# The last spectral block's sums on the PSUM banks of the side that was idle

## The chip, the core and the metric

The kernel runs on one core of one Trainium2 chip. The metric is the device time of one execution in microseconds (us); the time of a kernel is the median of several executions. Everything is float32, and large products are made as three products of a rounded part and a remainder ("hi" and "lo"), which the code calls `products` or writes out as `(hi, a), (hi, a's lo), (lo, a)`.

## What is computed

The input x has 2048 rows of 512 numbers. Two mixers read it and a gate blends them:

```python
g = sigmoid((x * gate_w).sum(-1, keepdims=True))
a = softmax(q @ k.T * scale) @ v, over 32 heads of 16, then @ wo     # A: attention
b = real(DFT_seq(DFT_hidden(x)))                                       # B: spectral
  = dft_seq_re @ (x @ dft_hid_re.T) - dft_seq_im @ (x @ dft_hid_im.T)
out = g * a + (1 - g) * b
```

## The kernel before, in words

The program has a front and a loop. The **front** projects x to queries, keys and values, makes the two spectral operands x @ dft_hid, and then multiplies them by the sequence matrices, one block of 128 output rows after the other. Beside this work it scans scores: for the softmax it needs the row maxima of q @ k.T, and the function `beside()`, called after every step of the front, puts a scan between the products at a chosen pace. The **loop** then runs over 16 pairs of heads with 32 steps each: scores, exp, and the product with the values.

The order of instructions on each engine is the order in which the code is written (nothing reorders it); waits are put in by the tile layer, which knows which tile lies where. TensorE (PE) is one stream in order: what waits there holds everything behind it. A step of the front is one pair of matmuls, one on rows 0 to 63 of the array and one on rows 64 to 127 (`halves_of`, L203), which run together and write to two PSUM banks.

PSUM has 8 banks, and in the front they are split so. Four of them on the right (numbers 4 to 7) hold scans. Once the front has reached its folded scans these are four tiles d0, d1, k0, k1 of one bank each. A folded scan (`scan_folded`, L172) writes one bank per half; of its two scores blocks ScalarE (ACT) copies one with Relu to SBUF (`fold`, L176) and VectorE (DVE) later reads the other with it and takes the maximum (L178). The bank is free for a new scan when ACT or DVE has read it.

The other four (numbers 0 to 3) hold the sums of the blocks, as two **sides** of two banks: side 0 and side 1. The function `xy()` gives each new block the other side: `turns[0] += 1; side = turns[0] % 2`. While block n accumulates on one side, block n-1 on the other is read out by ACT: `tx` (L767, one bank) and `ty` (the other bank), each multiplied by 1 - g. The read of `ty` is put 5 steps later for most blocks (L316); for the last block but one of the spectral part it stands straight behind `tx` (L769). From 12 to 44 steps after the end of a block the idle side serves as a third place for scans (`spare`, `bed`); after the last block but one it does not.

At the last spectral block the pool of the sides (`pxy`) is closed and the loop's pool (`psf`) takes the same four banks. The loop's pool has two tiles of two banks, `wide(0)` and `wide(1)`:

```python
if n == len(coef) - NU:
    sides.close()
    psf.append(ctx.enter_context(tc.tile_pool(name="psf", bufs=1, space=PSUM, ...)))
if u == 0:
    pss[t] = xy(n == len(coef) - NU)      # joined: wide(side)
```

A pool lays its tiles in PSUM in the order in which their tags are first asked for. The last block is side 0 by the count of turns (the code asserts it), so it asks for `wide(0)` first and gets banks 0 and 1. In the front the first call of `xy()` gives side 1, so in `pxy` side 1 lies on banks 0 and 1 and side 0 on banks 2 and 3. The last block but one is on side 1. In the last block the loop's first steps are already interleaved (`go_ahead`, at steps 30, 31, 37 and 44 of the 48): a memset of the sum bank, two scores blocks for exp and one scan; those that need two banks take `wide(1)`, banks 2 and 3.

Of the kernel before, what the change touches and what calls it, by code (L numbers as in the profile page):

```python
# [53 lines left out]
SCANS_IN = 0  # L54
# [12 lines left out]
def build(tc, xT, wqkv, wo, wrT, wiT, cr, ci, ct, gate, out):  # L67
    nc = tc.nc
    with ExitStack() as ctx:
# [199 lines left out]
        with ExitStack() as pf:  # L269
# [9 lines left out]
            def side_bank(side, j, name):  # L279
                return pxy.tile([P, 512], F32, tag=f"side{side}{j}", name=name)  # L280
# [126 lines left out]
            sides, banks = ExitStack(), ExitStack()  # L407
            pxy = sides.enter_context(tc.tile_pool(name="pxy", bufs=1, space=PSUM, reuse_waits="tile"))
            pss1.append(banks.enter_context(tc.tile_pool(name="pss1", bufs=2, space=PSUM, side="right")))

            def begin_folds():

                banks.close()
                psk.append(ctx.enter_context(tc.tile_pool(name="psk", bufs=1, space=PSUM, side="right", reuse_waits="tile")))
                beds.extend((bed, fp))
                scan_at(BESIDE)
# [941 lines left out]
```

## Time and profile before

| | us |
|---|---|
| median of 3 runs (lowest, highest) | 1718.13 (1718.02, 1718.69) |
| profiled execution, its own time | 1716.91 |
| its span, first to last instruction | 1715.1 |
| PE busy | 1701.1 |
| ACT busy | 1493.0 |
| DVE busy | 1186.8 |
| mean granted PE clock | 0.998 |

The front takes the first 665 us of the span, the loop the rest. In the rows of the profile a line is engine, line of the code, operation, written tile <- read tiles; bracketed at the end stand the engine's idle time before it and what ended it. Matmuls overlap, so the durations of PE rows (0.40 us for a single one) are longer than the distance between starts, and the distance is what counts. PEld is the load of the stationary operand of a matmul. PEclk is the clock granted to PE as a share of full speed.

### The profile page before, as it was taken

Reading aid. Unit: us, or ns where it says so; the run is one execution under the profiler, and the core shown is the slowest. Engines: PE = TensorE matmul, PEld = TensorE weight load, DVE = VectorE, ACT = ScalarE, POOL = GpSimd, SP = SyncE. Lnnn points to the kernel's source line nnn. Section 1 sums busy time; section 2 is a strip of 40 time slices with the busy share of each in tenths; the row PEclk is TensorE's granted clock in tenths of the full one; section 3 lists DMA queues with packets and bytes.
Section 4 is the critical chain, followed back from the end, with each engine's and each line's share of the span. In section 5 each row is a group of like instructions: output and inputs, shape, how many; then the busy total and the mean of one; then the engine's idle time right before and its main releaser. Section 6 shows DMA issues by size and latency. Waiting matters only on the chain.

```text
span 1715.1 us, 36307 instructions
## 1 busy us (share of the span) xinstructions
PE 1701.1 (99%) x13560; PEld 1030.1 (60%) x13560; DVE 1186.8 (69%) x2179; ACT 1493.0 (87%) x2472; POOL 765.0 (45%) x909
## 2 busy tenths in 40 slices
PE   9999999999999999999999999999999999999998
PEld 6988888988888795433333333333345555555554
DVE  5898888889899996666666666666642455654343
ACT  6447889888888887999999999999998888888876
POOL 3672435755555762433535455353422333334222
PEclk9999999999999999999999999999999999999999
DMA  7783457533337664256444445343436465575733
GB/s 255 243 289 76 149 161 216 161 112 107 104 110 204 175 134 95 83 131 153 136 112 113 121 114 135 99 124 85 93 76 145 131 149 148 140 172 157 192 93 127
DMA packets 148962, 240.96 MB, mean 140 GB/s; under 512 B 50049, under 2 KB 60785, under 8 KB 142193
## 3 DMA queue, kind: packets, MB, share of 16 engines
q1 hardware_dynamic: 133520, 217.27, 46.5%
q0 software_dynamic: 14688, 20.33, 5.0%
q8 instruction: 106, 1.74, 0.5%
q10 hardware_dynamic: 576, 1.05, 0.2%
q14 instruction: 72, 0.58, 0.1%
HBM read 158.34 MB, written 81.01 MB: 140 GB/s over the span
## 4 chain that ended last, share of the span: by engine, by line
PE 98%; ACT 0%; DMA 0%; DVE 0%; issue 0%; SPq 0%; DVEq 0%; ACTq 0%
PE pvb L804 29%; PE xy L203 26%; PE s L228 19%; PE s L172 9%; PE s L203 9%; PE s L153 5%; DMA raws<-wqkv 0%; PE s L593 0%; DVE y L919 0%; ACT fold L176 0%; DVE fold L178 0%; SPq L563 0%; SPq L562 0%; ACT ty L316 0%; PE s L1306 0%
## 5 line engine op out<-in xcount | busy, mean ns | idle before, releaser
L252 ACT ACTIVATE eb<-s 128x1024 f32<-128x1024 f32 x512 | 581.1, 1135 | 59.6 <-PE s L228 59.5
L260 ACT ACTIVATE e<-s 128x512 f32<-128x512 f32 x1022 | 610.6, 711 | 0.0
L155 DVE TENSOR_REDUCE mx<-s 128x2 f32<-128x1024 f32 x380 | 460.9, 1224 | 196.8 <-PE s L153 196.5
L804 PE MATMUL pvb<-eb,va 128*17 128x512 f32 x2052 | 514.4, 597 | 0.0
L804 PE MATMUL pvb<-e,va 128*17 128x512 f32 x2044 | 513.5, 597 | 0.0
L178 DVE CUSTOM_DVE_ANT_0 fold<-s,fold 128x512 f32<-128x512 f32 x644 | 433.2, 690 | 59.9 <-PE s L172 34.0
L176 ACT ACTIVATE fold<-s 128x512 f32<-128x512 f32 x644 | 377.8, 603 | 83.9 <-PE s L172 64.0
L228 PEld LDWEIGHTS s<-qs,ks 50*128 50x128 f32 x2048 | 214.6, 184 | 361.7 <-ACT eb L252 269.4
L228 PE MATMUL s<-qs,ks 50*128 50x512 f32 x2048 | 424.0, 435 | 0.0
L203 PE MATMUL xy<-b,c 64*128 64x512 f32 x2448 | 393.5, 394 | 2.0 <-ACT ty L769 1.7
L172 PE MATMUL s<-ks,qs 48*128 48x512 f32 x1288 | 315.2, 403 | 1.3 <-DVE mx L178 0.9
L203 PEld LDWEIGHTS xy<-b,c 64*128 64x128 f32 x2448 | 289.1, 187 | 29.2 <-POOL c L402 2.1
L172 PEld LDWEIGHTS s<-ks,qs 48*128 48x128 f32 x1288 | 171.6, 185 | 35.8 <-DVE mx L178 9.6
L804 PEld LDWEIGHTS pvb<-eb,va 128*17 128x17 f32 x2052 | 69.8, 96 | 188.8 <-issue 179.5
L153 PE MATMUL s<-ks,qs 48*128 48x512 f32 x760 | 156.0, 394 | 0.0
L203 PE MATMUL s<-b,b 64*128 64x512 f32 x1050 | 136.6, 391 | 0.0
L823 POOL DMA_DIRECT2D r_d<-lc x31 | 18.0, 580 | 264.6 <-DVE lc L822 216.9
L203 PE MATMUL xy<-w,b 64*128 64x512 f32 x768 | 115.0, 392 | 0.0
L816 POOL DMA_DIRECT2D lc<-ob x124 | 63.1, 515 | 115.9 <-DVE ob L813 110.6
L203 PEld LDWEIGHTS s<-b,b 64*128 64x128 f32 x1050 | 100.2, 185 | 23.6 <-issue 1.0
L403 POOL TENSOR_TENSOR c<-craw,c 128x512 fp32r<-128x512 f32 x84 | 110.2, 1312 | 6.7
L825 POOL DMA_DIRECT2D rb<-r_d x124 | 60.6, 496 | 102.0 <-DMA r_d<-lc 96.2
(149 smaller groups left out, 1563.1 us busy)
## 6 DMA issues: line engine op xcount, KB each, us to landing
qs<-q_d SPq DMA_DIRECT2D x68, 256.0 KB
craw<-cr SPq DMA_DIRECT2D x60, 256.0 KB
craw<-ct SPq DMA_DIRECT2D x48, 256.0 KB
ks<-k_d SPq DMA_DIRECT2D x46, 256.0 KB
kept_None<-sum SPq DMA_DIRECT2D x40, 256.0 KB
craw<-kept_None SPq DMA_DIRECT2D x40, 256.0 KB
qs<-q_d SPq DMA_DIRECT2D x68, 128.0 KB
craw<-ci SPq DMA_DIRECT2D x32, 256.0 KB
```

The costliest lines, as they stand in the source:

```text
L153: nc.tensor.matmul(ps[:, j, :], qs[b:b + 48, qb * P:(qb + 1) * P], ks[b:b + 48, c * 512:(c + 1) * 512], start=True, stop=True)
L155: nc.vector.tensor_reduce(mx[p][:, :, qb, c], ps, axis=AX.X, op=ALU.max)
L172: nc.tensor.matmul(ps, qs[b:b + 48, qb * P:(qb + 1) * P], ks[b:b + 48, c * 512:(c + 1) * 512], start=True, stop=True)
L176: nc.scalar.activation(fold[j], ps, AF.Relu)
L178: nc.vector.tensor_tensor_reduce(out=fold[j], in0=ps, in1=fold[j], scale=1.0, scalar=-3.0e38, op0=ALU.add, op1=ALU.max, accum_out=mx[p][:, ...
L203: nc.tensor.matmul(ps[j], lhs[r], rhs[r], start=first, stop=last)
L228: nc.tensor.matmul(pss[j], ks[b:b + 50, kb * P:(kb + 1) * P], qs[b:b + 50, q0:q0 + 512], start=True, stop=True)
L252: nc.scalar.activation(e, ps, AF.Exp, scale=SCALE)
L260: nc.scalar.activation(e[j], pss[j], AF.Exp, scale=SCALE)
L403: sub(lo, raw, hi.bitcast(F32))
L804: nc.tensor.matmul(pvb[r:r + VC, :], va[:, kb, 2 * p + j, :], es[c][j], start=kb == 0, stop=kb == NB - 1, tile_position=(0, r))
L816: nc.gpsimd.dma_start(lc[32 * n:32 * n + 32, :], ob[r + DH:r + VC, :].rearrange("p (s e) -> p s e", e=16))
```

## The change

Two lines are added where the front's pools are opened. They ask once for the two tiles of side 0 (SCANS_IN is 0), under a name that nothing writes or reads:

```diff
             pxy = sides.enter_context(tc.tile_pool(name="pxy", bufs=1, space=PSUM, reuse_waits="tile"))
             pss1.append(banks.enter_context(tc.tile_pool(name="pss1", bufs=2, space=PSUM, side="right")))
+            for j in range(2):
+                side_bank(SCANS_IN, j, "laid")
 
             def begin_folds():
```

with

```python
def side_bank(side, j, name):
    return pxy.tile([P, 512], F32, tag=f"side{side}{j}", name=name)
```

With that side 0 lies on banks 0 and 1 for the whole front and side 1 on banks 2 and 3. No instruction is added, removed or moved on any engine. Where the last block begins, the tile that its sums take over is no longer the one of the block just ended (side 1) but that of the block before it (side 0). All lines behind the two new ones have a number higher by two.

This is PE's stream before where the last block begins. `s` is a scan's bank, `xy` a block's sums, `b` a spectral operand, `c` a coefficient block; `Activation`, `DVE` and `Pool` are the semaphores of ACT, DVE and POOL. The second row is the last product of the block before, the third is the first of the last block.

```order
L172 MATMUL s<-ks,qs 128x512 [waits Activation_49]
L203 MATMUL xy<-b_9769,c 128x512 x2
L203 MATMUL xy<-b_9127,c 128x512 [waits Activation_49,Pool_49]
L203 MATMUL xy<-b_9127,c 128x512
L203 MATMUL xy<-b_9128,c 128x512 x2
L172 MATMUL s<-ks,qs 128x512
L172 MATMUL s<-ks,qs 128x512 [waits DVE_49]
L203 MATMUL xy<-b_9127,c 128x512 [waits Pool_49]
L203 MATMUL xy<-b_9127,c 128x512
L203 MATMUL xy<-b_9168,c 128x512 x2
L172 MATMUL s<-ks,qs 128x512 [waits DVE_49]
L172 MATMUL s<-ks,qs 128x512
```

The same place with the change:

```order
L172 MATMUL s<-ks,qs 128x512 [waits Activation_49]
L203 MATMUL xy<-b_9771,c 128x512 x2
L203 MATMUL xy<-b_9129,c 128x512 [waits Pool_49]
L203 MATMUL xy<-b_9129,c 128x512
L203 MATMUL xy<-b_9130,c 128x512 x2
L172 MATMUL s<-ks,qs 128x512 [waits Activation_49]
L172 MATMUL s<-ks,qs 128x512 [waits DVE_49]
L203 MATMUL xy<-b_9129,c 128x512 [waits Pool_49]
L203 MATMUL xy<-b_9129,c 128x512
L203 MATMUL xy<-b_9170,c 128x512 x2
L172 MATMUL s<-ks,qs 128x512 [waits DVE_49]
L172 MATMUL s<-ks,qs 128x512 [waits Activation_49]
```

The wait of the last block's first matmul for ACT (it was for `ty`, L769) is gone. The scan in the sixth row and the one in the last row now wait for ACT in their own name: for the copy that last read the scan's bank, which in the program before is older than `ty` and so was covered by the wait for it. These three rows of PE are all that differs in the program; on the other engines every row and every wait is the same.

## The prediction

> **What bounds the kernel now.** I read the page first: the busy times and the chain that ended last.
>
> ```profile
> PE 1701.1 (99%) x13560; PEld 1030.1 (60%) x13560; DVE 1186.8 (69%) x2179; ACT 1493.0 (87%) x2472; POOL 765.0 (45%) x909
> PE 98%; ACT 0%; DMA 0%; DVE 0%; issue 0%; SPq 0%; DVEq 0%; ACTq 0%
> ```
>
> PE carries the end: the chain runs through it for 98% of the span, and of 1715.1 us it idles 14. A change that removes one wait can pay only where PE itself waited. So the view of PE's waits was next (engine, line, what it waited for: us in total, times, longest).
>
> ```profile
> PE xy L203 <- ACT ty L769: 1.7, 1, 1.7
> PE s L172 <- DVE mx L178: 0.9, 3, 0.5
> ```
>
> The first row is the wait that the change takes out: it occurs once, and it is the longest single wait that PE has for another engine. Next I looked at its surroundings in stretches. The columns are the stretch, its length, then each engine's busy us with its instructions, PE's granted clock, the DMA share and GB/s.
>
> ```profile
> 636.00:646.20 10.20, 10.20 (x91) 8.40 (x88) 9.45 (x29) 8.33 (x14) 5.27 (x6) 1.00 0.77 109
> 646.20:648.20 2.00, 0.35 (x4) 0.00 (x0) 0.96 (x4) 1.81 (x4) 1.48 (x2) 1.00 0.35 69
> 648.20:649.40 1.20, 1.12 (x9) 1.09 (x11) 0.00 (x0) 0.14 (x1) 1.20 (x2) 0.92 1.00 355
> 649.40:652.40 3.00, 3.00 (x17) 2.82 (x15) 1.88 (x5) 1.65 (x3) 1.73 (x2) 0.50 0.31 120
> 652.40:656.00 3.60, 3.60 (x32) 3.04 (x28) 2.98 (x10) 2.40 (x4) 0.00 (x0) 0.97 0.11 39
> 656.00:664.00 8.00, 8.00 (x69) 7.56 (x71) 3.02 (x6) 2.70 (x5) 0.00 (x0) 1.00 0.01 2
> ```
>
> The reader is to see the clock, third column from the right. It is full before the stall and through it, and about 1 us after PE starts again it falls to 0.50 for some 3 us. So the stall has a second price: matmuls that run at half speed after it. PE's own rows show both.
>
> ```profile
> 645.22 0.40 PE L172 MATMUL s<-ks,qs 48*128 48x512 f32 x2
> ...
> 645.92 0.41 PE L172 MATMUL s<-ks,qs 48*128 48x512 f32 x2
> 646.16 0.40 PE L203 MATMUL xy<-b,c 64*128 64x512 f32 x2
> 648.28 0.74 PE L203 MATMUL xy<-b,c 64*128 64x512 f32 x4 [1.73 <-ACT ty L769]
> 648.82 0.44 PE L172 MATMUL s<-ks,qs 48*128 48x512 f32 x2
> ...
> 649.79 0.70 PE L172 MATMUL s<-ks,qs 48*128 48x512 f32 x2
> ...
> 651.07 0.70 PE L172 MATMUL s<-ks,qs 48*128 48x512 f32 x2
> ...
> 652.35 0.56 PE L172 MATMUL s<-ks,qs 48*128 48x512 f32 x2
> ...
> 653.17 0.43 PE L172 MATMUL s<-ks,qs 48*128 48x512 f32 x2
> ...
> 655.50 0.93 PE L172 MATMUL s<-ks,qs 48*128 48x512 f32 x3
> 655.94 1.21 PE L203 MATMUL xy<-b,c 64*128 64x512 f32 x7
> ```
>
> From 645.22 to 645.92 PE does three pairs (one of a scan, two of the block): 0.70 us, so 0.235 us a pair. The scans of the last block should follow each other at that 0.705; after the stall their distances are 0.97, 1.28, 1.28 and 0.82.
>
> **The change, part by part.** The two new calls issue nothing, so they cost nothing, on any queue; the only tiles whose place differs are the blocks' sums and the scans lent to their sides, and they change places with each other. What remains is one wait of PE.
>
> *Taken away, the stall.* The pair at 646.16 would be followed at 646.40 by the next; it came at 648.28. That is 1.88 us. It need not wait for anything else there: side 0 had no scan in the last 4 steps of the block before, and the coefficient it reads was prepared three units earlier.
>
> *Taken away, the slow clock.* Against 0.705 the four distances hold 0.27 + 0.58 + 0.58 + 0.12 = 1.53 us.
>
> [...]
>
> *Added, waits of the scans.* The stall also let ACT and DVE catch up; without it they become the limit for a while. ACT's rows, at an earlier end of a block and at this one:
>
> ```profile
> 632.14 0.71 ACT L316 ACTIVATE ty<-xy,gm 128x512 f32<-128x512 f32 x1
> 632.71 3.21 ACT L176 ACTIVATE fold<-s 128x512 f32<-128x512 f32 x5
> ...
> 642.84 4.14 ACT L176 ACTIVATE fold<-s 128x512 f32<-128x512 f32 x6 [0.31 <-PE s L172]
> 646.88 0.68 ACT L767 ACTIVATE tx<-xy,gm 128x512 f32<-128x512 f32 x1
> 647.45 0.69 ACT L769 ACTIVATE ty<-xy,gm 128x512 f32<-128x512 f32 x1
> 649.26 0.60 ACT L176 ACTIVATE fold<-s 128x512 f32<-128x512 f32 x1 [1.12 <-PE s L172]
> ```
>
> `tx` starts at 646.88 behind a fold, so it stays there, and so does `ty` at 647.45. Without the stall the first scan of the last block runs at 646.40 + 2 x 0.235 = 646.87, the second at 647.57; the ACT copies that they newly wait for are the last two of the six that begin at 642.84 and end at 646.98, so these two waits cost nothing. The third scan, due at 648.28, reuses the first one's banks: its fold follows `ty` after 0.57 (as 632.14 to 632.71), at 648.02, and ends 0.60 later at 648.62. ACT to PE takes 0.14 (`ty` ends at 648.14, PE starts at 648.28), so this scan starts at 648.76, 0.48 late. From there DVE is the chain:
>
> ```profile
> 630.92 0.69 DVE L178 CUSTOM_DVE_ANT_0 fold<-s,fold 128x512 f32<-128x512 f32 x1
> ...
> 634.06 0.69 DVE L178 CUSTOM_DVE_ANT_0 fold<-s,fold 128x512 f32<-128x512 f32 x1
> ...
> 646.46 0.69 DVE L178 CUSTOM_DVE_ANT_0 fold<-s,fold 128x512 f32<-128x512 f32 x1
> ...
> 649.41 0.69 DVE L178 CUSTOM_DVE_ANT_0 fold<-s,fold 128x512 f32<-128x512 f32 x1 [2.25 <-PE s L172]
> ...
> 653.01 0.69 DVE L178 CUSTOM_DVE_ANT_0 fold<-s,fold 128x512 f32<-128x512 f32 x1 [0.40 <-PE s L172]
> ...
> 655.18 0.69 DVE L178 CUSTOM_DVE_ANT_0 fold<-s,fold 128x512 f32<-128x512 f32 x1
> 655.93 0.18 PEld L172 LDWEIGHTS s<-ks,qs 48*128 48x128 f32 x1 [0.40 <-DVE mx L178]
> ```
>
> When it is fed without gaps DVE takes three of these in 2.17 us (653.01 to 655.18), 0.72 each. DVE is idle from the fold at 646.46 to the one at 649.41, the last block's first. The last scan of the front, at 655.93, waits for the block's seventh, the one at 655.18. Without the stall the second fold decides: it needs ACT's copy that ends at 648.62, so it starts at 648.66 (the first has run before, from 647.3 on). Five more distances of 0.72 bring the seventh to 652.26; it lasts 0.69, and with 0.15 to PE the last scan starts at 653.1. With no wait of PE at all it would start after 17 pairs of the block and 8 of scans: 646.40 + 25 x 0.235 = 652.28. So the new waits hold 0.8 us, spread over 6 us in pieces of at most 0.5.
>
> *The sum.* 655.93 - 653.1 = **2.8 us** earlier; by terms, 1.88 (stall) + 1.53 (clock) + 0.2 (what the old wait at 655.93 held) - 0.8 (new waits). The bounds: 655.93 - 652.28 = 3.65 if ACT and DVE are never late; and 2.5 if DVE goes at the slower pace that it had behind the end of the block before, four distances in 3.14 us (630.92 to 634.06), 0.785 each, which puts the seventh fold 0.33 later. I take 2.8, since its durations are those of the same place.
>
> *What carries it to the end.* From 655.94 on PE runs 8.00 of 8.00 us, so the block's end moves by the same amount. The loop then:
>
> ```profile
> 659.96 1.03 ACT L252 ACTIVATE eb<-s 128x1024 f32<-128x1024 f32 x1 [3.35 <-PE s L228]
> ...
> 663.90 1.02 ACT L252 ACTIVATE eb<-s 128x1024 f32<-128x1024 f32 x1 [1.94 <-PE s L228]
> ...
> 666.26 1.02 ACT L252 ACTIVATE eb<-s 128x1024 f32<-128x1024 f32 x1 [0.35 <-PE s L228]
> ...
> 700.00:800.00 100.00, 100.00 (x742) 38.15 (x740) 67.57 (x63) 100.00 (x160) 45.59 (x61) 1.00 0.49 129
> ```
>
> ACT enters it waiting for PE three times, and is busy without a gap later (100.00 of 100 us), so its stream of exps starts earlier by what PE is earlier. The first two banks of the loop now lie where `ty` was read; that read ends at 648.14, and PE needs them at about 656.5. Nothing gives the 2.8 us back.
>
> The profiled execution took 1716.91 us and its span 1715.1; it would take 1714.1. The median of the runs lies 1.22 above it, and the same difference from 1718.13 gives **1715.3 us**. A measurement of this kernel tells about 0.2%, 3.4 us, from no change, so this forecast counts as no change by a little.
>
> **The rivals.**
>
> *More: the drop of the clock is larger in the timed runs.* The profiled execution is 1.22 us faster than their median. If that is a longer drop behind the same stall, the change removes it too: 2.8 + 1.2 = 4.0, 1714.1 us. For it: nothing else in the program waits by chance at a cost of this size. Against it: a profiled execution can differ in other ways.
>
> *Less: in the timed runs the clock does not drop.* Then PE goes at 0.235 from 648.28 and DVE decides before as well: from its first fold at 649.41 six distances of 0.72 lead to the seventh at 653.73, and 0.69 + 0.15 later, at 654.57, the last scan starts. The gain is 654.57 - 653.1 = 1.5: 1716.6 us. [...]
>
> *Slower: the loop's first scores wait for their rows.* The first exp's scores now start near 656.5, and they need rows whose loads were issued by the queue up to 646. If those landed late, PE would wait there; it is a loss over 0.2% if they land later than 659.3 + 3.4 = 662.7.
>
> ```profile
> 654.00:656.00 2.00, 2.00 (x20) 1.59 (x16) 1.81 (x6) 1.41 (x3) 0.00 (x0) 1.00 0.01 4
> ```
>
> The DMA share is 0.01 by 654, so they have long landed. A chance of 0.03.
>
> *Nothing: the span does not follow PE's start,* or the removed wait was not the one that held PE: 1718.1 us.
>
> **How the numbers follow.** The forecast (2.5 to 3.65 us less) 0.55; larger drop 0.22; no drop 0.15; slower 0.03; nothing 0.05. Over 0.2% faster are the larger drop and the upper tail of the forecast (0.10): 0.32. Slower 0.04 with 0.01 for what I don't see. The rest, 0.64, is within. The range goes from the larger drop with 0.2 of spread, 1713.9, to the case without a drop with 0.3, 1716.9; outside lie slower, nothing, and a part of the larger drop, some 0.15 together.
>
> **What would show it.** In the new profile the wait of PE for `ty` is gone from PE's waits; PEclk is 1.00 in every stretch from 636 to 664; the third scan of the last block waits about 0.5 us for ACT's fold and the last one for DVE; the first exp starts at about 657.2 instead of 659.96, and the span is about 1712.3. I am wrong if PE stalls again within the block for more than 1 us, if the clock drops all the same, or if the exp stream starts earlier and the span doesn't follow.

## The result, and the profile after

The changed kernel takes 1714.35 us (median of 22 executions, 1713.49 to 1715.53) and the kernel before 1717.01 us (22 executions beside them, 1715.36 to 1718.69). The ratio is 0.9986 with a 95% interval of 0.998 to 0.9992: a gain of 2.7 us, which is clear of the scatter and below 0.2%. Forecast were 1715.3 us and a gain of 2.8; the 1715.3 were counted from 1718.13, the median of three, and the same gain counted from 1717.01 is 1714.2. The profiled execution's span is 1712.4 us; 1712.3 was forecast.

PE's waits after, all that the view lists:

```profile
PE s L580 <- POOL ident masks.py:199: 1.4, 1, 1.4
PE s L172 <- DVE mx L178: 0.9, 3, 0.4
PE s L1308 <- DVE rb L1305: 0.9, 1, 0.9
PE s L172 <- ACT fold L176: 0.6, 2, 0.4
PE xy L203 <- ACT c L371: 0.3, 1, 0.3
PE xy L203 <- DVE b L372: 0.2, 1, 0.2
```

The wait for `ty` is gone, and a scan that waits for ACT's fold has come. The same stretches as before the change (stretch, length, busy us of each engine with its instructions, PEclk, DMA share, GB/s):

```profile
646.20:648.20 2.00, 2.00 (x20) 1.59 (x16) 1.73 (x6) 1.86 (x5) 1.41 (x2) 1.00 0.05 6
648.20:649.40 1.20, 0.95 (x10) 0.49 (x6) 0.68 (x2) 1.10 (x4) 1.20 (x2) 1.00 0.57 171
649.40:652.40 3.00, 3.00 (x29) 2.52 (x27) 2.93 (x11) 2.57 (x5) 1.86 (x2) 1.00 0.52 194
```

PE is busy through the place of the stall and the clock is full in all of it: where the kernel before did 17 matmuls in 3.00 us, 29 are done. PE, DVE and ACT in order of time:

```profile
646.22 0.87 PE L203 MATMUL xy<-b,c 64*128 64x512 f32 x6
646.92 0.40 PE L172 MATMUL s<-ks,qs 48*128 48x512 f32 x2
...
647.62 0.41 PE L172 MATMUL s<-ks,qs 48*128 48x512 f32 x2
...
648.74 0.50 PE L172 MATMUL s<-ks,qs 48*128 48x512 f32 x2 [0.25 <-ACT fold L176]
...
653.01 3.69 PE L203 MATMUL xy<-b,c 64*128 64x512 f32 x28
656.32 0.61 PE L228 MATMUL s<-qs,ks 50*128 50x512 f32 x2
```

```profile
648.72 0.69 DVE L178 CUSTOM_DVE_ANT_0 fold<-s,fold 128x512 f32<-128x512 f32 x1 [0.52 <-ACT fold L176]
...
652.25 0.69 DVE L178 CUSTOM_DVE_ANT_0 fold<-s,fold 128x512 f32<-128x512 f32 x1
```

```profile
657.03 1.03 ACT L252 ACTIVATE eb<-s 128x1024 f32<-128x1024 f32 x1 [3.35 <-PE s L228]
...
660.96 1.02 ACT L252 ACTIVATE eb<-s 128x1024 f32<-128x1024 f32 x1 [1.93 <-PE s L228]
...
663.31 1.02 ACT L252 ACTIVATE eb<-s 128x1024 f32<-128x1024 f32 x1 [0.35 <-PE s L228]
```

The third scan starts at 648.74, DVE's second fold at 648.72 and its seventh at 652.25, the front's last scan goes with the row at 653.01, and the first exp starts at 657.03 instead of 659.96. The three waits of ACT at the loop's entry are those of before (3.35, 1.93, 0.35), only 2.9 us earlier.

One measure serves for all that follows, since the front of an execution can end up to 0.9 us later than in another: the time from the last pair of the block before to the first scores of the loop. It is 659.29 - 646.16 = 13.13 us before and 656.32 - 646.22 = 10.10 us after.

### The profile page after: what moved, and what is told of

Read it like the earlier page. It is cut to its first block, busy times and chain, and to the rows that moved or that the text cites. A ratio compares the mean times of both kernels' runs of the same rounds, so it can differ in the third digit from the quotient of the medians.

```text
span 1712.4 us, 36306 instructions
## 1 busy us (share of the span) xinstructions
PE 1701.0 (99%) x13560; PEld 1022.5 (60%) x13560; DVE 1188.9 (69%) x2179; ACT 1492.3 (87%) x2472; POOL 765.4 (45%) x909
## 4 chain that ended last, share of the span: by engine, by line
PE 97%; DMA 1%; DVE 0%; issue 0%; ACT 0%; SPq 0%; DVEq 0%; ACTq 0%
PE pvb L806 29%; PE xy L203 26%; PE s L228 19%; PE s L172 9%; PE s L203 8%; PE s L153 5%; DMA q_d<-eh 0%; DMA raws<-wqkv 0%; DMA raws<-xT 0%; PE s L595 0%; DVE y L921 0%; DVE fold L178 0%; ACT fold L176 0%; SPq L565 0%; SPq L564 0%
## 5 line engine op out<-in xcount | busy, mean ns | idle before, releaser
L203 PEld LDWEIGHTS xy<-b,c 64*128 64x128 f32 x2448 | 284.0, 187 | 30.5 <-issue 1.0
```

What stands on the lines that cost most here:

```text
L203: nc.tensor.matmul(ps[j], lhs[r], rhs[r], start=first, stop=last)
```

## The experiments

My theory: what counts is which block's banks the last block takes over, and the stall that this causes is paid twice, as idle time and as a slower clock. The rivals: the new place of the sides pays by itself; the clock falls for another reason; what is left of waits is PE's own pace.

### Which part of the new placement counts

The loop's two tiles can be laid in the other order, with the change (e1) and without it (e2):

```diff
     psf.append(ctx.enter_context(tc.tile_pool(name="psf", ...)))
+    wide(1 - SCANS_IN, "laid")
```

> The changed kernel, with the loop's two tiles laid in the other order too, so that the last block's sums again lie on the banks of the block just ended (now banks 2 and 3). My theory (what counts is which block's banks the last block takes over): PE waits 1.7 us for ty again, the clock falls to 0.50 behind it for about 3 us, the first exp starts at about 660.0 us of the span, the span is about 1715.1 and the time that of the kernel before, ratio 1.000. Rival (where the sides lie in the front pays in itself): the time of the changed kernel, ratio 0.9985.

> The kernel before, with only the loop's two tiles laid in the other order: the front's sides stay where they were, the last block takes banks 2 and 3, those of side 0. My theory: the same as the changed kernel, no wait for ty, PEclk 1.00 all through, first exp at about 657.0, span 1712.4, ratio 0.9985. Rival (the front's placement pays): the kernel before, span 1715.1, ratio 1.000.

e1 took 1716.96 us (ratio to the kernel before 0.9999, 0.999 to 1.0008), e2 1714.82 us (0.999, 0.9981 to 0.9998). So the front's placement pays nothing by itself that these intervals show, and the loop's order alone does what the change does. e2's measure is 657.02 - 646.91 = 10.11 us, as after; its span is 1713.0 us where 1712.4 was expected, and its front ended 0.7 us later than the changed kernel's (646.91 against 646.22). e1 has the wait back:

```profile
PE xy L203 <- ACT ty L772: 1.7, 1, 1.7
```

but not all of the expectation came true. Its clock:

```profile
646.20:648.20 2.00, 0.52 (x6) 0.09 (x2) 1.12 (x4) 1.85 (x4) 1.30 (x2) 1.00 0.05 6
648.20:649.40 1.20, 0.96 (x8) 0.96 (x10) 0.00 (x0) 0.10 (x1) 1.20 (x2) 1.00 0.54 117
649.40:652.40 3.00, 3.00 (x29) 2.78 (x27) 2.72 (x8) 2.55 (x5) 1.83 (x2) 1.00 0.62 216
```

The same stall of 1.7 us, and in this execution the clock did not fall; by their mean clock 5 of e1's 11 executions lost it. Its measure is 657.87 - 646.31 = 11.56 us. Against 13.13 in the kernel before, 1.57 us are the price of the fall when it happens; against 10.11, 1.45 us are the price of the stall without it. Whether the clock falls differs from one execution to the next.

### How often the clock falls, and what decides it

Each execution has its mean granted clock. At the span's end PE idles and the clock falls in every trace, 1.9 to 5.3 us before the last instruction, so an undisturbed execution shows 0.999 (at the far end of that range 0.998), and one fall of 3.4 us more makes 0.998 or 0.997 of it. The rounding makes single cases uncertain, but few: of the 77 executions of the changed kernel, e2, e4, e5 and e8, none of which has the stall of 1.7 us, one shows 0.998. Of the 80 executions of the kernel before that ran beside the experiments, 44 show 0.998 or 0.997, with a median of 1717.7 us, and 36 show 0.999, with a median of 1716.3 us. They ran on two chips: 33 of 65 on one, and 11 of 15 on the one that e7 below ran on. Of the 33 of the changed kernel (22, and 11 as e9 below) none is below 0.999.

The first try to measure the clock's part by itself put seven extra pairs of matmuls ahead of the last block, to keep PE busy while it would wait:

```diff
     psf.append(ctx.enter_context(tc.tile_pool(name="psf", ...)))
+    busy = wide(1 - SCANS_IN, "busy")
+    for _ in range(7):
+        halves_of((busy[:, 0, :], busy[:, 1, :]), hi[:, 0, :], ah[0], True, True)
```

> The kernel before with seven extra pairs of matmuls ahead of the last block (7 x 0.235 = 1.65 us, on the loop's other tile, read by nobody), so that PE is busy while it would wait for ty. It measures the clock's part by itself. My theory (the idling makes the clock fall): PE waits only about 0.2 us for ty, PEclk stays 1.00, the last block starts at 648.3 as before, the front's last scan at about 654.6 instead of 655.9, first exp at about 658.6, span about 1713.7, so 1.4 us of the 2.8 come without any change of banks, ratio 0.9992. Rival (the clock falls there for another reason, or its fall costs nothing): PEclk 0.50 again, last scan at 655.9, span 1715.1, ratio 1.000.

It missed by its own construction: the extra tile was asked for first, so it, and not the block, got the banks of the block just ended, and the extra pairs waited for `ty`.

```profile
PE busy L203 <- ACT ty L772: 1.7, 1, 1.7
649.40:652.40 3.00, 3.00 (x17) 2.90 (x16) 0.28 (x1) 0.48 (x1) 1.60 (x2) 0.50 0.50 188
```

1717.52 us (1.0003, 0.9994 to 1.0012): the stall stayed and work was added. It shows again that the first tile asked for takes the stall. It does not part the clock from the stall: the clock fell as in the kernel before, in 5 of 11 executions by the mean. Put right, with the block's tile laid first:

```diff
     psf.append(ctx.enter_context(tc.tile_pool(name="psf", ...)))
+    wide(SCANS_IN, "laid")
+    busy = wide(1 - SCANS_IN, "busy")
+    for _ in range(7):
+        halves_of((busy[:, 0, :], busy[:, 1, :]), hi[:, 0, :], ah[0], True, True)
```

> The filler of e3 put right: the tile of the last block is laid first, so the seven extra pairs write banks 2 and 3, which are idle, and wait for nothing. The block still waits for ty, but PE is busy for 1.65 us of that time. My theory (idling makes the clock fall in a part of the executions, here never): every execution has a mean clock of 0.999, none of 0.998; their times lie where the undisturbed half of the kernel before lies, median about 1715.8; 11.5 us from the last pair of the block before to the first scores of the loop, like e1, whose clock did not fall. Rival (the clock falls there by chance of another kind): about half of the executions at 0.998 and above 1716.8.

1715.57 us (0.9991, 0.9982 to 1.0): 1.3 us below the median of the kernel before beside it (1716.83), with more work and the same late start of the block; the interval reaches 1.0. One execution took 4081.99 us, for a cause that the record does not show; without it the median is 1715.51. PE's rows in the filled stall, then the stretch behind it and the stretch at the span's end (columns as in the other stretches):

```profile
647.03 0.40 PE L203 MATMUL xy<-b,c 64*128 64x512 f32 x2
647.27 1.77 PE L203 MATMUL busy<-b,c 64*128 64x512 f32 x14
649.07 0.74 PE L203 MATMUL xy<-b,c 64*128 64x512 f32 x4
...
658.55 0.58 PE L228 MATMUL s<-qs,ks 50*128 50x512 f32 x2
649.40:652.40 3.00, 3.00 (x28) 2.42 (x25) 2.12 (x7) 1.95 (x4) 2.66 (x3) 1.00 0.00 0
1708.99:1714.25 5.26, 0.00 (x0) 0.00 (x0) 0.14 (x1) 0.00 (x0) 0.01 (x1) 0.50 0.67 250
```

The measure is 11.52 us, as in e1, whose clock stayed up by luck. Of the ten other executions nine show 0.999; the one at 0.998 is the profiled one, and its clock is full in every stretch from 636 to 664: it lost its thousandth at the span's end, where the fall began 5.3 us before the last instruction, the most of all traces. So behind the filled stall none of the ten is known to have fallen, where 15 of the 32 of the kernel before beside them show one. The block starts as late as before and only the idling is gone: by these counts it is the idling that lets the clock fall.

Then the length of the stall. Shorter, without the copy `ty`, and longer, with the copy made twice:

```diff
     if n == len(coef) - NU - 1:
-        nc.scalar.mul(ty, pss[t][1], gm[:, t:t + 1])
+        ty = tx
```

```diff
     if n == len(coef) - NU - 1:
         nc.scalar.mul(ty, pss[t][1], gm[:, t:t + 1])
+        nc.scalar.mul(ty, pss[t][1], gm[:, t:t + 1])
```

> The kernel before, with the copy ty of the last block but one left out (tx is added in its place, so that this block's output rows are wrong): the last block waits for tx alone, a stall of 1.3 us with 1.15 us of idling instead of 1.88 with 1.72. My theory (the clock falls where the idling fills about half of a stretch of 3.4 us that starts at a time of its own: 18 of 33 executions for 1.72 us put that bound at about 1.6 us): no execution at 0.998, PEclk 1.00, median about 1715.2. Rival (any stall over 1 us does it in half of the executions): about 6 of 11 at 0.998, and a spread of 3 us.

> The kernel before, with the copy ty of the last block but one made twice, so that the last block waits 0.57 us longer: a stall of 2.45 us with 2.3 us of idling. By the same theory as for e8 (bound about 1.6 us of idling in a stretch of 3.4 us): about 7 in 10 executions at a mean clock of 0.998 or lower, about 8 of 11; those without the drop at about 1716.3, the others 2 us later. Rival (the length of the stall does not matter): half of them.

```profile
PE xy L203 <- ACT tx L767: 1.1, 1, 1.1
648.20:652.40 4.20, 4.20 (x38) 3.67 (x39) 3.17 (x9) 2.96 (x5) 2.43 (x3) 1.00 0.59 188
```

```profile
PE xy L203 <- ACT ty L770: 2.4, 1, 2.4
649.40:652.40 3.00, 2.91 (x14) 2.55 (x16) 0.70 (x2) 0.60 (x1) 2.55 (x2) 0.52 0.00 0
```

e8 (first fence) idles 1.1 us and no execution of 11 is below 0.999: 1715.35 us (0.9992, 0.9983 to 1.0001), scattered over 1.5 us. e7 idles 2.4 us and 9 of 11 are below: 1717.99 us (1.0004, 0.9995 to 1.0013). So of executions that idle 1.1, 1.7 and 2.4 us there, 0 of 11, 44 of 80 and 9 of 11 lose the clock. A fall at random, whatever the stall's length, is excluded by e8, against 33 of 65 of the kernel before on the same chip. e7 by its count says little, since the kernel before beside it fell in 11 of 15; its two executions without a fall lie at 1717.1 us, where 1716.3 was expected.

The traces say more than the counts, for each lists every change of PE's clock. In the kernel before, e3 and e7 the fall lasts 3.413 us each time, and from it to the fall at the span's end there are 311, 312 and 311 times 3.413 us. So in these three traces the changes of the clock lie on a raster of stretches of 3.413 us. It does not begin with the program: the fall begins 649.20 us after the first instruction in the kernel before and 649.50 in e7. In e1 and e8, where no earlier fall came, I take the raster to be the same and lay it backwards from the fall at the span's end. Here are the stretch of the raster that holds most of the idle time, and the next one, for the kernel before, e7, e1 and e8 in this order:

```profile
645.79:649.20 3.41, 1.68 (x16) 1.24 (x14) 1.36 (x4) 2.22 (x4) 2.48 (x3) 1.00 0.50 143
649.20:652.61 3.41, 3.41 (x20) 3.20 (x18) 2.09 (x6) 1.79 (x3) 1.93 (x2) 0.50 0.39 151
646.09:649.50 3.41, 0.96 (x11) 0.38 (x8) 1.52 (x6) 3.04 (x5) 1.95 (x3) 1.00 0.63 222
649.50:652.91 3.41, 3.41 (x16) 2.96 (x18) 1.08 (x3) 1.05 (x2) 2.47 (x2) 0.50 0.01 2
647.07:650.48 3.41, 2.04 (x18) 2.04 (x20) 1.16 (x5) 2.14 (x5) 2.86 (x3) 1.00 0.50 139
650.48:653.89 3.41, 3.41 (x32) 3.17 (x31) 3.24 (x11) 2.93 (x6) 1.30 (x1) 1.00 0.41 156
646.09:649.50 3.41, 2.31 (x20) 1.73 (x18) 1.75 (x7) 2.20 (x4) 2.38 (x3) 1.00 0.21 44
649.50:652.91 3.41, 3.41 (x32) 2.91 (x31) 3.34 (x11) 2.85 (x6) 1.64 (x2) 1.00 0.66 213
```

With 1.73 us of a stretch idle (3.41 less PE's 1.68) the clock is at 0.50 for the whole next stretch, and so it is with 2.45 in e7. In e1 the raster, laid so, cuts the same stall in two, 0.35 us and 1.37, and the clock stays at 1.00, as with 1.10 in e8. The rest of the kernel before agrees: between the span's start and the fall at its end only one other stretch of its raster holds more than 0.9 us of idling of PE, the last one (1707.33 to 1710.74, 2.86 us), and the clock is at 0.50 behind it too. So by these traces, as an estimate, the bound lies between 1.37 and 1.73 us of idling in one stretch of 3.41 (1.6 was worked out beforehand), and how the stall falls across the stretches differs between executions. If every place of the raster is equally likely, the chance of a fall is by this, as an estimate, 49% to 70% for 1.73 us and 70% to 92% for 2.45; 44 of 80 and 9 of 11 were counted.

### What is left of the new waits

Two ways to give the scans more room in the last block, both on the changed kernel. The side of the block just ended as a third place for scans:

```diff
+    lent = {}
...
+    if at == "w" and psf:
+        if j == 0:
+            lent[n] = wide(side, "s")
+        return lent[n][:, j, :]
...
     if 0 < t < NB - 3 and n < len(coef) - NU - 1:
         spare[:] = side_of[t], slots[0] + 12, slots[0] + 44
+    if n == len(coef) - NU - 1:
+        spare[:] = side_of[t], slots[0] + 6, slots[0] + 28
```

> The changed kernel, with the side of the block just ended lent to scans from step 6 to step 28 of the last block, as a third place beside d and k (in the other blocks this is done from step 12 to 44 of the next block). It takes away what is left of the new waits. My theory (the scan that waits for ACT's fold does so for want of a bank): the third scan of the last block starts at 648.3 to 648.4 instead of 648.74, the last one at about 652.4 instead of 653.0, the first exp at about 656.5, the span about 0.5 us below the changed kernel's, 1711.9, ratio 0.9982; the difference to the changed kernel is below what times can show, the trace decides. Rival (DVE's chain of folds is the limit whatever the banks): last scan at 653.0, span 1712.4.

1715.26 us (0.9989, 0.9981 to 0.9998), no better than the change. The third scan no longer holds PE, but the next one waits for ACT's fold, and a later one for DVE:

```profile
PE s L172 <- DVE mx L178: 0.3, 1, 0.3
PE s L172 <- ACT fold L176: 0.3, 1, 0.3
```

Its measure is 656.83 - 646.38 = 10.45 us, above the 10.10 of the change. So the theory that a bank was wanting is wrong: a bank more did not help, since the readers of the banks were late all the same. The rival is not shown either, for it expected no loss, and DVE itself idled for PE before two of its folds (0.42 and 0.70 us). What makes this order of scans slower stays open. And the scans further apart, at the same work:

```diff
     psf.append(ctx.enter_context(tc.tile_pool(name="psf", ...)))
+    scan_at(2.7)
```

with the changed kernel itself beside it:

> The changed kernel, with the scans of the last block set 2.7 steps apart instead of 2.15 (the last scan still comes before step 30). The same work, and only the new waits are taken away. My theory (the new waits hold PE about 0.8 us because ACT and DVE cannot keep the pace behind tx and ty): only the third scan still waits, about 0.25 us for ACT's fold; from the last pair of the block before to the first scores of the loop 9.6 us instead of 10.10, span and time about 0.5 us below the changed kernel's, PEclk 1.00. Rival (PE is the limit there and the waits are only shown as such): 10.1 us, no difference.

> The changed kernel itself, for a comparison with e5 on the same chip: 10.1 us from the last pair of the block before to the first scores of the loop, median 1714.3 to 1714.8, every mean clock 0.999.

```profile
646.45 0.85 PE L203 MATMUL xy<-b,c 64*128 64x512 f32 x6
...
648.97 0.50 PE L172 MATMUL s<-ks,qs 48*128 48x512 f32 x2
...
656.35 0.61 PE L228 MATMUL s<-qs,ks 50*128 50x512 f32 x2
```

e5 took 1714.53 us (0.9986, 0.9976 to 0.9995), e9 1714.95 us (0.999, 0.9981 to 0.9999). The measure is 9.90 us against 10.10 in e9: 0.2 us less, where 0.5 was expected. In the times the two cannot be told apart. What the new waits hold in all can be read from e8 and e1, which have a stall but no fall: less the stall (648.04 - 646.54 and 648.44 - 646.31, each less one pair of 0.235) their measures are 9.64 and 9.67 us. The changed kernel's 10.10 is about 0.45 above that, and e5 takes away 0.2 of it.

## Why the prediction was right

**The stall.** Removed, at the place and of the length that the prediction named; e1 and e2 show that it hangs on which block's banks are taken over and on nothing else of the placement.

**The slow clock.** The size of one fall was right: 1.53 us forecast, 1.57 between the profiled executions with and without it. What the prediction had wrong is that it took the fall of one profiled execution for that of all. It happens in about half of them (44 of 80). The case "the clock does not drop", put beside the forecast as a rival with a chance of 0.15, is therefore not a rival but the other half of the same kernel (its gain of 1.5 us is what e1 has above the changed kernel: 11.56 - 10.10 = 1.46); the median of the kernel before lies between the two halves (36 executions around 1716.3 us, 44 around 1717.7), and that the forecast met the median's gain so closely is in part luck, owed to this mixture: between the two profiled executions the measure differs by 3.03 us, and between median executions by 2.7. The mixture goes with the wider scatter, 3.3 us before and 2.0 us after over 22 executions each, but does not account for all of it: the 36 at 0.999 alone lie 2.8 us apart.

**The new waits.** The chain was the one forecast: the third scan at 648.74 (648.76 forecast), DVE's second and seventh folds at 648.72 and 652.25 (648.66 and 652.26). The sum of 0.8 us was too large. Up to the last scan it is 653.01 - (646.46 + 25 x 0.235) = 0.68 us, so this scan starts 2.92 us earlier (655.93 to 653.01) where 2.8 was forecast; up to the first scores of the loop, which the prediction did not part from it, only about 0.45 us are left.

**What carries it to the end.** The first exp is 2.93 us earlier, the span 2.7. The two tenths between are lost in the loop; no wait that took them stands out, and single executions differ by more: from the first scores to the span's end the profiled ones take 1055.7 to 1056.5 us.

**The rivals.** *Larger drop*: the three runs shown before were among the five slowest of 22, and the two halves of the kernel before lie 1.4 us apart, no more than the fall that was profiled costs; so nothing points to a larger drop, though its 1714.1 us lies nearer to the measured 1714.35 than the forecast's 1715.3. *Slower* and *nothing* did not occur: the first scores of the loop waited for no load.

## What to carry to other kernels

When one pool takes over the PSUM banks of another, look which tile of the old pool each new one lands on: here a tile that started on the banks of work just ended waited 1.7 us for their reader, one on the idle banks did not (e1 against the changed kernel, the kernel before against e2), and one line that asks for a tile early was enough to swap them. Look at PE's clock behind a stall before pricing it at its length alone: in this kernel the clock fell behind 1.7 us of idling in 44 executions of 80 and behind 1.1 us in none of 11, and one fall cost 1.57 us beside the 1.45 of the stall. One profile did not tell how often (e1's shows full clock, and 5 of its 11 executions fell); the mean clock of each execution did. The scatter between executions was wider with the stall, 3.3 us against 2.0, though the falls do not account for all of it.

## What the runs showed of the hardware

Idling of 1.7 us was enough to halve PE's clock for 3.413 us, and the same program did it in 44 executions of 80 and not in the others, while 1.1 us of idling did it in none of 11 and 2.4 us in 9 of 11; I had not expected that. By the traces of the kernel before, e7, e1 and e8, what decides is how much of one stretch of 3.413 us is idle: 1.73 and 2.45 us were enough, 1.37 and 1.10 were not. Nor had I expected that matmuls whose result nobody reads, put into the stall, keep the clock up (none of ten executions is known to have fallen behind them, 15 of 32 beside them did) and make the kernel no slower (1715.57 against 1716.83 us, ratio 0.9982 to 1.0).
